# Routed attention and a tanh-shrink feed-forward on one core: third pair's sums copied ahead of weight conversions, list work placed behind weight pieces, products of zeros moved within the prologue

## The chip, the cores and the metric

The kernel runs on one core of a Trainium2 chip. The metric is the device time of one execution in microseconds (us). All times of the trace below are counted from the start of the span of one profiled execution.

## The reference

```python
# q, k, v: (4, 8, 768, 64); centroids: (8, 16, 64); w_in: (512, 2048); w_out: (2048, 512)
q_assign = argmax(einsum('bhsd,hcd->bhsc', q_n, c_n))      # nearest of 16 centroids, normalised
k_assign = argmax(einsum('bhsd,hcd->bhsc', k_n, c_n))
mask = q_assign[:, :, :, None] == k_assign[:, :, None, :]
scores = where(mask, matmul(q, k^T) / sqrt(64), -1e9)
attn = softmax(scores)
x = matmul(attn, v), heads side by side: (3072, 512)
h = x @ w_in
out = (h - tanh(h)) @ w_out
```

The weights arrive as 64-bit floats, two 32-bit words a number, and are converted on the chip.

## The kernel before

Two heads make a pair; there are 4 pairs in each of 4 batches, n = 0 to 15. A pair's 768 queries are cut into two halves of 384, and its 768 keys into three steps s of 256. The main loop runs over 96 such steps (n, half, s): first half 0 of pairs 0 to 3 (steps 0 to 11), then half 1 of the same pairs (12 to 23), then pairs 4 to 15 with both halves in turn. In each step TensorE (PE) makes the scores of the *next* step (`sc`, L451), ScalarE (ACT) takes their exponentials (L473), VectorE (DVE) masks them where the mask isn't already in the product (L483), and PE multiplies with v (`av`, L505). In steps 0 to 11 PE has no feed-forward work; from step 12 the feed-forward of what is finished is dealt out between the steps (`h`, L626; `o`, L642; later `pu`, L818 and `pd`, L869, a seven-product scheme).

The order on every engine is the order in which the Python code issues instructions; nothing reorders it afterwards. Within a step, work that isn't TensorE's main stream is collected in a list `todo`, and `between()` issues it in equal shares between the feed-forward items of the step.

The mask of pairs 1 to 3 in half 0 is a product too (L462) with two one-hot tiles `hot`. To get them, the cluster codes of a pair (`route`, from `pr` L364) are transposed (`pq`, L396), written to memory (`q_codes`, SyncE's queue, SP, L402), read back into 128 partitions (`hot`, L418) and compared on DVE (L426, L430). For unmasked steps the codes come back as `row` (L409), which the masking on DVE (L483) reads.

A half of a pair needs the sums of its weights. `total` copies them from PSUM to a tile `den` on ACT (L544). From there two ways lead on:

- Pairs for which `soon(n)` holds (the third and fourth of the first batch, and the fourth of each other): PE multiplies `den` by a matrix that picks one row out (`tally`, L598, in `pick`, first batch's half 0), DVE takes reciprocals (L603) and scales `xT` (L606).
- The others go through memory, in stages of later steps: `total` also writes the sums (`list`, SP, L553); one step on `compact` reads them as 128x6 (`each`, `other`, L566); two steps on `invert` adds and inverts on DVE (L574, L575) and writes `back` (L577); three steps on `spread_out` reads `back` into `den` (L582); five steps on `scale` multiplies `xT` on DVE (L588). For pair 1's half 0 the last three come a step later. These stages stand in a dictionary `later` by step.

The weights come in 32 pieces. GpSimd (POOL) fetches a raw piece (L218), three ahead; `rest_of` prepares half of its words on ACT (L149, L150) and `round_piece` puts a piece together on DVE (L158, L161) and fetches the piece three on. `paces` says how many pieces a step takes. `rest` has two buffers, so that a third `rest_of` waits for the DVE conversion of the piece before the last.

In step 8, (2, 0, 2), the sums of pair 2's half 0 are complete. Before the change `take` (L530) and two `rest_of` are issued first, and `total` of pair 2 only with `todo`.

In the prologue `keep_warm(times)` issues products of zeros (L302), two instructions each on PE, which nothing reads.

Of the kernel before, what the change touches and what calls it, by code (L numbers as in the profile page):

```python
# [58 lines left out]
def kernel(  # L59
# [119 lines left out]
    def fast():  # L179
# [118 lines left out]
        def keep_warm(times: int):  # L298

            ps = ps_f.tile([P, 2 * P], F32, name="warm", tag="f")  # L300
            for _ in range(times):
                nc.tensor.matmul(  # L302
                    ps, lhsT=inverses[:, 0:P], rhs=inverses[:, 0 : 2 * P], start=True, stop=True
                )
# [22 lines left out]
        def turn(n: int, i: int, engine):  # L327

            pt = ps_s.tile([P, 2, 512], F32, name="pt", tag="s")
            x = raw_qk.pop((n, i))  # L330
            for j in range(NCH):
                nc.tensor.transpose(  # L332
                    out=pt[:, j // HCH, (j % HCH) * P : (j % HCH + 1) * P],
                    in_=x[:, j].rearrange("p h d -> p (h d)"), identity=ident,
                )
            pool = turnp0 if n in (2, 3) else turnp
            t = turned[n, i] = pool.tile([P, 2, TB], F32, name=f"t{i}")
            if engine is nc.scalar:
                nc.scalar.copy(out=t, in_=pt[:, :, 0:TB])
            else:  # L340
                nc.vector.tensor_copy(out=t, in_=pt[:, :, 0:TB])
# [49 lines left out]
        def publish(n: int):  # L391

            sides = 2 if masked(n, 0) else 1
            G = HCH * 4 * sides
            ps = ps_f.tile([G, P], F32, name="pq", tag="f")
            nc.tensor.transpose(  # L396
                out=ps, in_=codes[n][:, 0:sides].rearrange("p i a h j -> p (i a h j)"), identity=ident
            )
            t = rtp.tile([G, P], BF16, name=f"qc{sides}")
            nc.vector.tensor_copy(out=t, in_=ps)  # L400
            q_codes[n] = dram.tile([sides, 2, 2, HCH * P], BF16, name=f"q_codes{sides}")
            nc.sync.dma_start(q_codes[n].rearrange("i a h (j p) -> (i a h j) p", p=P), t)  # L402
# [591 lines left out]
        centroid_load()  # L994
        load(0)
        constants()
        keep_warm(9)
        centroid_norms()

        gate = const.tile([P, 1], F32, name="gate")  # L1000
# [9 lines left out]
        route(0)  # L1010
        turn(1, 0, nc.scalar)
        turn(1, 1, nc.scalar)
        publish(0)
        spread(0, 0)
        rest_of(0)
        similar(1)
        load(2)
        rest_of(1)

# [22 lines left out]


        paces = dict(enumerate((0, 0, 1, 1, 1, 0, 2, 1, 2, 1, 1, 0, 3, 2, 2, 2, 2, 2, 2, 3, 2)))
        late, divides, makers, later = [], [], [], {}
        fill, whole, spent, since, over = [], 0.0, 0.0, 0, 1
        for at, (n, half, s) in enumerate(steps):
            b, p = pairs[n]
            following = steps[at + 1] if at + 1 < len(steps) else None
            after = steps[at + 2] if at + 2 < len(steps) else None  # L1050
            if at == 4 * HALF:
                open_late()
            if at == 4 * HALF - 9:
                open_stream()
            if at in fills:
                fill, over = fills[at][0](), fills[at][1]
                whole, spent, since = sum(it[0] for it in fill), 0.0, at
            if at == 2 * HALF:
                makers = [it for i in range(2) for it in up_maker(i)]
                makers += [it for i in range(2) for it in down_maker(i)]  # L1060
            now = []
            part = (at - since + 1) / over
            while fill and (spent + fill[0][0] / 2 <= whole * part or part == 1):
                now.append(fill.pop(0))
                spent += now[-1][0]
            stages = ready.get(at, {})

            values_first = 1 in stages and not summed(n, half)
            if values_first:
                value(n, half, s)  # L1070
            if 1 in stages:
                stages[1]()
            if after and after[2] == 0 and not masked(*after[:2]):
                spread(*after[:2])
            if following and at >= NS - 1:
                begin(following)
            while picks:
                picks.pop(0)()
            share = paces.get(at, 0)
            todays, rounding = rounding[:share], rounding[share:]  # L1080
            taken = summed(n, half) and s == NS - 1
            if not taken:
                for piece in todays[:2]:
                    rest_of(piece)
            if not values_first:
                value(n, half, s)
            if summed(n, half):
                if 0 in stages:
                    stages.pop(0)()
                sum_up(n, half, s)  # L1090
            if s == NS - 1:
                take(n, half)
                if taken:
                    for piece in todays[:2]:
                        rest_of(piece)
                if soon(n):
                    if summed(n, half):
                        picks.append(lambda n=n, half=half: pick(n, half))
                    divides = [lambda n=n, half=half, i=i: divide(n, half, i) for i in range(HCH)]
                else:  # L1100

                    slow = int((n, half) == (1, 0))
                    for i, stage in (
                        (0, total), (1, compact), (2 + slow, invert), (3 + slow, spread_out),
                        (5 + slow, scale),
                    ):
                        later.setdefault(at + i, []).append(
                            lambda stage=stage, n=n, half=half: stage(n, half)
                        )

                if p == HP - 1 and (half == 1 or b == 0):
                    total(n, half)
                    if summed(n, half):
                        picks += divides
                    else:
                        late += divides
                    divides = []
                if (n, half) == (HP - 1, 0):
                    load(HP)
                if half == 1:  # L1120
                    load(n + (HP if n < 2 else 2), (2,) if n < 2 or n >= HP else ())

            todo = []
            if following:
                todo += [lambda i=i: select(*following[:2], 2 * following[2] + i) for i in range(2)]
            todo += [stages[i] for i in (5, 3, 4, 2) if i in stages]
            todo += late + later.pop(at, [])
            late = []
            if divides:
                todo.append(lambda n=n, half=half: total(n, half))  # L1130
                late, divides = divides, []
            for i, piece in enumerate(todays):
                todo.append(lambda piece=piece: round_piece(piece))
                if i == 0:
                    todo += [lambda piece=piece: rest_of(piece) for piece in todays[2:]]

            light = [i for i in range(at, 4 * HALF - 2) if i % 3 and i % 6 != 1]
            if makers and at in light:
                share = -(-len(makers) // len(light))
                todo += makers[:share]  # L1140
                del makers[:share]
            if "raw" in late_pools:
                todo += [check_done, check_done, check_on, check_on]
                if p == HP - 1 and half == 1 and s == NS - 2:
                    todo += [lambda b=b, c=c: right_factors(b, c) for c in range(CH - 1)]
            slots = max(sum(it[1] for it in now), 1)
            place = iter(range(slots))
            turned_at = max(slots - 1 - now[-1][1], 0) if now else 0

            def between():  # L1150
                i = next(place)
                for it in todo[i * len(todo) // slots : (i + 1) * len(todo) // slots]:
                    it()

                if i == turned_at and 0 in stages:
                    stages[0]()

            if at in fills and "raw" in late_pools:
                for c in range(CH - 1 if at > 4 * HALF else 0, CH):
                    right_factors(b - 1, c)  # L1160
            for it in now:
                it[2](between)
            if not now:
                between()
# [225 lines left out]
```

## Time and profile before

| what | value |
|---|---|
| device time, 3 executions | 987.56, 988.15, 988.5 us; median 988.15 |
| profiled execution | 992.2 us; span of its instructions 990.4 us |
| PE busy | 978.1 us, 99% of the span |
| DVE, ACT, POOL busy | 532.0, 322.0, 499.6 us |
| mean granted TensorE clock | 0.995 |
| mean memory traffic | 134 GB/s |

The slices of the whole span (each digit the busy tenths of one of 40 slices, 24.8 us each) show that PE is full from end to end:

```
PE   8999999999999999999999999999999999999997
DVE  5457557448656667656554357655645336533011
ACT  5566564333442323243331222324341221122000
POOL 1025334444445464776777345676688345466600
PEclk9999999999999999999999999999999999999999
DMA  7656353025475724463536737344453232233231
```

The change touches the first four slices, up to about 90 us, and the order of small work in all later steps. The steps of interest begin, by the scores that they issue for the step after them, at 60.4 us (step 8), 64.9 us (step 9), 73.4 us (step 10), 77.4 us (step 11) and 81.1 us (step 12).

### The profile page before, as it was taken

The page shows a single profiled execution, that of the slowest core. Times are in us where ns is not written, and L with a number is a line of the kernel's source. Part 1 is how long each engine was busy: PE and PEld are TensorE (multiplying, and loading weights), DVE is VectorE, ACT ScalarE, POOL GpSimd, SP SyncE. Part 2 cuts the span into 40 slices and gives each one's busy share as a digit, 9 for nine tenths or more (in the row PEclk, how much of TensorE's full clock was granted, in tenths as well). Part 3 has the DMA queues.
Part 4 walks back from the last instruction along what each step waited for, and adds up shares of the span by engine and source line. Part 5 has one row for each costly group of instructions (what it writes and reads, how often), then busy time and mean ns, then how long its engine had stood idle before and what let it go on. Part 6 is the DMA issues. An engine that isn't in the chain of part 4 may idle for free.

```text
span 990.4 us, 16604 instructions
## 1 busy us (share of the span) xinstructions
PE 978.1 (99%) x6452; PEld 465.8 (47%) x6452; DVE 532.0 (54%) x1019; ACT 322.0 (33%) x493; POOL 499.6 (50%) x347
## 2 busy tenths in 40 slices
PE   8999999999999999999999999999999999999997
PEld 5433443344443334444455555444455555444664
DVE  5457557448656667656554357655645336533011
ACT  5566564333442323243331222324341221122000
POOL 1025334444445464776777345676688345466600
PEclk9999999999999999999999999999999999999999
DMA  7656353025475724463536737344453232233231
GB/s 201 182 143 172 111 177 108 30 51 152 118 222 133 228 92 125 147 174 117 174 113 195 200 116 216 109 147 124 149 166 93 101 110 73 104 112 127 103 102 35
DMA packets 115977, 132.47 MB, mean 134 GB/s; under 512 B 62980, under 2 KB 95668, under 8 KB 113204
## 3 DMA queue, kind: packets, MB, share of 16 engines
q1 hardware_dynamic: 109508, 109.81, 37.5%
q0 software_dynamic: 6240, 21.50, 6.5%
q8 instruction: 53, 0.87, 0.4%
q14 instruction: 32, 0.26, 0.1%
q10 hardware_dynamic: 144, 0.03, 0.0%
HBM read 110.14 MB, written 21.17 MB: 133 GB/s over the span
## 4 chain that ended last, share of the span: by engine, by line
PE 96%; DVE 1%; DMA 1%; ACT 0%; issue 0%; SPq 0%; ACTq 0%; DVEq 0%
PE pd L869 22%; PE pu L818 21%; PE sc L451 14%; PE av L505 14%; PE o L642 8%; PE h L626 8%; PE pt L332 2%; PE den L539 2%; PE sim L351 1%; PE warm L302 1%; DMA den<-back 1%; PE den L520 1%; PE pr L364 1%; DVE e L483 0%; PE pq L396 0%; DMA q_codes<-qc 0%
## 5 line engine op out<-in xcount | busy, mean ns | idle before, releaser
L496 POOL TENSOR_TENSOR sum<-sum,e 128x768 f32<-128x768 f32 x112 | 206.1, 1840 | 106.5 <-DVE e L483 102.7
L483 DVE SCALAR_TENSOR_TENSOR e<-row,code,sc 128x384 f32<-128x384 bf16 x336 | 185.2, 607 | 97.2 <-ACT sc L473 74.3
L869 PE MATMUL pd<-stream,G 128*64 128x256 f32 x1728 | 191.8, 379 | 0.0
L473 ACT ACTIVATE sc<-sc 128x768 f32<-128x768 f32 x168 | 125.8, 792 | 202.3 <-PE sc L451 187.9
L869 PEld LDWEIGHTS pd<-stream,G 128*64 128x64 f32 x1728 | 123.7, 137 | 67.4 <-issue 7.9
L451 PE MATMUL sc<-t,t 64*128 64x384 f32 x768 | 151.5, 513 | 0.1
L505 PE MATMUL av<-e,vals 128*64 128x384 f32 x768 | 146.4, 501 | 0.0
L813 POOL TENSOR_TENSOR G<-G,th 128x768 f32<-128x768 f32 (+1 forms) x51 | 88.0, 1739 | 98.7 <-ACT th L811 98.7
L818 PE MATMUL pu<-xT,stream 128*64 128x384 f32 x768 | 134.9, 488 | 0.7 <-DVE top L372 0.7
L818 PE MATMUL pu<-diff,stream 128*64 128x384 f32 x576 | 103.1, 487 | 0.0
L451 PEld LDWEIGHTS sc<-t,t 64*128 64x128 f32 x768 | 66.6, 188 | 74.6 <-issue 41.7
L492 POOL TENSOR_TENSOR sum<-e 128x768 f32<-128x768 f32 x28 | 56.8, 2029 | 75.8 <-DVE e L483 67.5
L818 PEld LDWEIGHTS pu<-xT,stream 128*64 128x64 f32 x768 | 54.1, 137 | 69.6 <-issue 62.2
L505 PEld LDWEIGHTS av<-e,vals 128*64 128x64 f32 x768 | 47.8, 137 | 82.7 <-issue 80.8
L626 PE MATMUL h<-xT,w_in 128*64 128x384 f32 x512 | 86.3, 487 | 0.0
L642 PE MATMUL o<-w_out,g 128*64 128x512 f32 x384 | 86.3, 594 | 0.0
L811 ACT ACTIVATE th<-G 128x768 f32<-128x768 f32 (+1 forms) x51 | 40.8, 805 | 117.9 <-DVE G L806 112.1
L818 PEld LDWEIGHTS pu<-diff,stream 128*64 128x64 f32 x576 | 40.7, 137 | 49.9 <-issue 44.5
L806 DVE TENSOR_TENSOR G<-pu,u 128x384 f32<-128x384 f32 x72 | 39.7, 552 | 41.4 <-PE pu L818 41.2
L626 PEld LDWEIGHTS h<-xT,w_in 128*64 128x64 f32 x512 | 36.4, 137 | 46.2 <-issue 45.1
L642 PEld LDWEIGHTS o<-w_out,g 128*64 128x64 f32 x384 | 27.0, 137 | 50.3 <-issue 49.6
L880 DVE SCALAR_TENSOR_TENSOR c<-pd,du 128x256 f32<-128x256 f32 x36 | 15.1, 420 | 62.9 <-PE pd L869 62.9
(127 smaller groups left out, 840.7 us busy)
## 6 DMA issues: line engine op xcount, KB each, us to landing
stream<-up_factors SPq DMA_DIRECT2D x24, 896.0 KB
stream<-down_factors SPq DMA_DIRECT2D x21, 1024.0 KB
raw<-in_moe_w_in_dram POOLq DMA_DIRECT2D x16, 512.0 KB, 6.1
raw<-in_moe_w_out_dram POOLq DMA_DIRECT2D x16, 512.0 KB, 5.0
again<-in_moe_w_in_dram SPq DMA_DIRECT2D x32, 256.0 KB
again<-in_moe_w_out_dram SPq DMA_DIRECT2D x32, 256.0 KB
x<-in_q_dram SPq DMA_DIRECT2D x32, 192.0 KB
x<-in_k_dram SPq DMA_DIRECT2D x32, 192.0 KB
```

The source lines that it names most:

```text
L451: nc.tensor.matmul(sc[i][:, h, 0:TB], lhsT=turned[n, 1][r].rearrange("p a n -> p (a n)")[:, j * P : (j + 1) * P], rhs=turned[n, 0][r, half ...
L473: nc.scalar.activation(out=out, in_=sc[i][:, :, 0:TB], func=ACT.Exp, scale=SCALE)
L483: nc.vector.scalar_tensor_tensor(out=e[:, h], in0=rows[n, half][:, h], scalar=codes[n][:, 1, j // HCH, h, j % HCH : j % HCH + 1], in1=sc[: ...
L492: nc.gpsimd.tensor_tensor(out=s, in0=pair[0], in1=pair[1], op=ALU.add)
L496: nc.gpsimd.tensor_tensor(out=s, in0=s, in1=pair[i], op=ALU.add)
L505: nc.tensor.matmul(avs[n, half][h * D : h * D + D], lhsT=vals[n][:, h, j], rhs=e[i][:, h], start=(j == 0), stop=(j == NCH - 1),)
L626: nc.tensor.matmul(h[r], lhsT=w_in[i][:, c, o * P : (o + 1) * P][:, r], rhs=xT[c][:, half], start=(c == 0), stop=(c == CD - 1),)
L642: nc.tensor.matmul(acc[sub][r], lhsT=gs[f % HF][:, f // HF, sub * P : (sub + 1) * P][:, r], rhs=w_out[f // FQ][:, f % FQ], start=(f == seq ...
L811: nc.scalar.activation(out=th, in_=t, func=ACT.Tanh)
L813: nc.gpsimd.tensor_tensor(out=t, in0=t, in1=th, op=ALU.subtract)
L818: nc.tensor.matmul(ps[r], lhsT=streams[base + i][:, c, k_, r], rhs=right[c], start=(c == 0), stop=(c == CH - 1),)
L869: nc.tensor.matmul(ps[r], lhsT=left(i)[:, r], rhs=t[:, i], start=(i == 0), stop=(i == HF - 1))
```

## The change

Three parts, in the prologue and in the main loop.

1. In step 8, where `taken` and `soon(n)` hold, `total` is issued directly behind `take`, ahead of the two `rest_of` that follow. `total` of the step is then not put into `todo` again. (For step 11 the call moves within the same block, without other instructions between.)
2. The stages of `later` are split: `total` (stage 0) stays at its place in `todo`; `compact`, `invert`, `spread_out` and `scale` go to a list `listed` that is appended behind the step's `round_piece` calls.
3. `keep_warm(9)` becomes `keep_warm(7)`; `keep_warm(3)` is added between the transposes of pair 1 and `publish(0)`, and `keep_warm(1)` behind `similar(1)`.

```diff
         constants()
-        keep_warm(9)
+        keep_warm(7)
         centroid_norms()
...
         turn(1, 1, nc.scalar)
+        keep_warm(3)
         publish(0)
         spread(0, 0)
         rest_of(0)
         similar(1)
+        keep_warm(1)
         load(2)
...
-            taken = summed(n, half) and s == NS - 1
+            taken = s == NS - 1 and summed(n, half)
...
                 if taken:
+                    if soon(n):
+                        total(n, half)
                     for piece in todays[:2]:
                         rest_of(piece)
...
                 if p == HP - 1 and (half == 1 or b == 0):
-                    total(n, half)
                     if summed(n, half):
                         picks += divides
                     else:
+                        total(n, half)
                         late += divides
                     divides = []
...
-            todo += late + later.pop(at, [])
+            todo += late
             late = []
             if divides:
-                todo.append(lambda n=n, half=half: total(n, half))
+                if not taken:
+                    todo.append(lambda n=n, half=half: total(n, half))
                 late, divides = divides, []
+
+            for it in later.pop(at, []):
+                if it[0] == 0:
+                    todo.append(it[1])
+                else:
+                    listed.append(it[1])
             for i, piece in enumerate(todays):
                 todo.append(lambda piece=piece: round_piece(piece))
                 if i == 0:
                     todo += [lambda piece=piece: rest_of(piece) for piece in todays[2:]]
+            todo += listed
+            listed = []
```

Beside the intended moves the order of instructions differs thus: on SP, for 17 of the 22 halves that go through memory, the two reads of `back` (L582) now stand behind the writes of the next half's `list` (L553) in place of ahead of them; on PE the product `den` (L539) stands one feed-forward item earlier in five places; on DVE `invert` and `scale` of the first batch stand behind one to three conversions. POOL's order is the same. PE executes two products of zeros (four instructions) more in all.

More of the change, by code (lines that the diff above doesn't have):

```diff
@@ L1044, in fast @@
         paces = dict(enumerate((0, 0, 1, 1, 1, 0, 2, 1, 2, 1, 1, 0, 3, 2, 2, 2, 2, 2, 2, 3, 2)))
-        late, divides, makers, later = [], [], [], {}
+        late, divides, makers, later, listed = [], [], [], {}, []
         fill, whole, spent, since, over = [], 0.0, 0.0, 0, 1
@@ L1107, in fast @@
                         later.setdefault(at + i, []).append(
-                            lambda stage=stage, n=n, half=half: stage(n, half)
+                            (i, lambda stage=stage, n=n, half=half: stage(n, half))
                         )
                 if p == HP - 1 and (half == 1 or b == 0):
-                    total(n, half)
                     if summed(n, half):
```

## Prediction

> **What bounds the kernel now.** I read the engine table first (PE busy 978.1 of 990.4 us), then the chain of waits and PE's own waits. The kernel is a TensorE stream; only places where PE stands still or runs slowly can give time back.
>
> ```profile
> PE 96%; DVE 1%; DMA 1%; ACT 0%; issue 0%; SPq 0%; ACTq 0%; DVEq 0%
> ...
> PE tally L598 <- ACT den L544: 2.0, 1, 2.0
> PE warm L302 <- DVE inverses L231: 1.3, 1, 1.3
> PE pq L396 <- DVE code L377: 1.2, 1, 1.2
> PE pu L818 <- DVE top L372: 0.7, 2, 0.3
> PE pr L364 <- ACT simt L356: 0.7, 1, 0.7
> ```
>
> The second block names who PE waited for (sum, count, longest in us): three waits can be won, 2.0 at the third pair's `tally`, 1.2 and 0.7 in the prologue. The chain of waits, in order of time (start, length), shows what stands behind the first:
>
> ```profile
> 57.78 7.32 DMA den<-back
> ...
> 65.19 0.56 DVE xT L588
> ...
> 68.35 0.34 ACT den L544
> ...
> 68.73 1.37 PE tally L598 x4
> 70.11 2.57 PE av L505 x8
> 72.68 0.78 PE den L520 x8
> 73.46 1.49 PE sc L451 x8
> ...
> 82.70 0.79 PE tally L598 x4
> 83.50 1.44 PE av L505 x8
> ```
>
> A list read (`den<-back`) holds DVE at `scale` of pair 0 until 65.19; the conversions behind it come late; ACT's second `rest_of` waits for a buffer; `den` of pair 2 stands behind it on ACT, and PE behind `den`. The last two rows are the same PE work undisturbed: after the wait it ran 0.58 and 1.13 us longer. Four stretches of one clock window each say why (busy PE, granted clock):
>
> ```profile
> 14.34:17.75 3.41, 1.55 (x14) 1.00 0.13 50
> 17.75:21.16 3.41, 3.41 (x13) 0.50 0.47 124
> 65.54:68.95 3.41, 1.43 (x12) 1.00 0.24 65
> 68.95:72.37 3.42, 3.42 (x12) 0.50 0.58 149
> ```
>
> A window in which PE idled 1.86 or 1.98 of 3.41 us was followed by one at half clock.
>
> [...] PE's `den` product had ended at 64.93 (64.08 + 0.85), yet ACT copied it at 68.22. [...] a `row` read issued at 71.97 landed only at 78.55, behind raw pieces that landed at 75.6 and 77.3; an undisturbed one took 17.64 to 20.79.
>
> **The change part by part**, against the span of 990.4.
>
> *Third pair's sums.* ACT's order becomes xT (to 64.68), `den`, then the two `rest_of`. `den` can run at 64.97 to 65.45. PE's next scores end at 66.75, so `tally` waits for nothing: 1.98 us gone, and with it the half clock, 0.58 + 1.13. Together 3.7 us here (`sc` of step 10 at 69.8, not 73.5). The `rest_of` behind it start 0.45 later (65.46, not 65.01); the exponentials queued behind them, which free the banks for `sc`, come at 68.3 instead of 68.58, because the second `rest_of` no longer waits 0.54 for DVE. They end at 69.8, just as PE arrives. So this part gains 2.0 where the half-clock window is missing, 3.7 where it is not. [...] Mean: 1.99 + 0.5 x 1.71 = 2.85.
>
> *List work behind weight pieces.* On DVE the conversion of step 7 runs at 62.2 to 63.4 inside the 3.04 us in which DVE waited for the list. What it costs: `den<-back` of pair 0 is issued behind four `list` writes (1.26 us on SP), so about 58.4 instead of 57.13; `scale` starts at 65.2 to 66.4 (both bounds: nothing later, as the DMA engines were full of raw pieces until 64, or the whole 1.26), I take 65.8. Nobody but the feed-forward at 84.8 needs it. Pair 1's `invert` then comes behind two conversions, the second of which waits for ACT (68.15): conversions end at 68.9, `back` is issued at 69.4, not 67.24. SP waits for its landing (3.5 us before), then issues `den<-back`, then `row` for step 12: about 74.2 instead of 71.97. This `row` matters. Step 12's four maskings (2.2), `scale` (0.55), three reciprocals (2.57) and xT (0.56) follow it on DVE, 5.95 us, and the fourth product group of the first `h` needs that xT, 86.79 before. With PE earlier by g, `row` must have landed by 86.79 - 5.95 - g = 80.8 - g, i.e. 78.0 for g = 2.85. When does it land? Earliest 74.2 + 3.15 = 77.4 (the undisturbed latency), latest 74.2 + 6.6 = 80.8 (the latency of before). The raw pieces in its way are fetched some 1.5 us earlier than before, since conversions are, so I take 78.3. That is a stall of 0.3 at the mean; as lateness costs and earliness gives nothing, I charge 0.8. Net of both parts: 2.85 - 0.85 = 2.0.
>
> The other 17 moved `den<-back` reads go behind `list`, which waits for ACT; `scale` follows two steps, over 16 us, later (the steps' scores lie 8 to 10 us apart), and the slowest read took 7.3. Cost nothing, hidden by the feed-forward. Behind them on SP stand loads that stood behind `list` anyway. The five `den` products that move up one item (1.29 or 3.4 us) read sums that POOL had finished 2.7 us or more before: nothing. POOL keeps its order.
>
> *Products of zeros.* The rows show starts 0.427 us apart for an instruction while cold and 0.21 once warm. Two products fewer are four instructions; the last began at 8.14 and `pc` at 8.36; now the stream ends at 7.46, `pc`'s inputs being there at 7.01 and the k load at 7.07: 0.9 earlier here. With windows elsewhere the gain lies between 0 (early warm, `pc` waits for its inputs) and 1.3; mean 0.5. The three products before `pq` are 6 x 0.213 = 1.28 us in a gap of 1.205: `pq` may come 0.1 late. If PE were cold there, 2.56, late by 1.4. The one behind `sim` takes 0.43 of a gap of 0.66: nothing. In exchange the half-clock window at 17.75 goes: `sc` took 2.89 where others take 1.49, `pr` 0.65 for 0.48, so 1.57. [...] Mean of the part: 0.5 - 0.1 + 0.14 x 1.57 = 0.6. In this very trace it would be 2.4, of which the one-hot read limits some: `hot` landed at 32.57 and PE met it at 33.6, while its codes queue behind loads that move only 0.75.
>
> *Sum.* 2.0 + 0.6 = 2.6 us. The profiled span (990.4) and execution (992.2) lie above the three timed ones (987.56 to 988.5), perhaps with more half-clock windows; that is why I use means over positions. 988.15 - 2.6 = 985.5.
>
> **Rivals.** About 0.2% (2.0 us) is what can be told from no change.
>
> A, likeliest: the wait goes, a part comes back at `row`. 985.5; its own range 983.8 to 986.5. Chance 0.60.
>
> B, the wait moves: `row` lands at 79.5 or later and PE stops 1.5 at the first `h`, or the three products delay `pq` by 1.4. Gain 2.85 - 1.5 + 0.6 - 0.9 (half of the clock's 1.71, if that hole is taken for idleness too) = 1.05: 987.1. For it: 1.5 us of SP and DVE work really moves ahead of `row`, and before it `row` had only 0.7 us to spare (78.55, masking at 79.28). Against: raw pieces move away from it. Chance 0.24.
>
> C, nothing comes back and both half-clock windows were there: 3.7 + 1.3 = 5.0, so 983.2. Against: the timed runs are below the profiled one. Chance 0.10.
>
> D, slower: the same `row`, pushed behind a raw piece, lands at 82 or later. PE then waits 82 - 77.1 = 4.9 at `h` (with g = 3.7), idles over 1.86 in a window, and the next 3.41 us at half clock cost 1.7: 6.6 lost against 3.7 + 0.6 won, 990.4. It decides from about 79.7, where stall and clock equal the gain, and is slower by more than 0.2% from 81.7. Against: 82 is 7.8 us after the issue, more than any read of this kind took. Chance 0.06.
>
> That the change doesn't do what it says is inside B: the products may not lie in idle time.
>
> **Numbers.** Faster by over 0.2%: 0.55 of A, all of C, 0.02 of B = 0.67; within: 0.05 of A, 0.22 of B = 0.27; slower 0.06. Range 983.0 to 987.5: it takes A, half of C and most of B, leaving out about 0.15. All cases but D have one sign.
>
> **What would show it.** PE's waits no longer list `tally` on ACT `den`; `den` of pair 2 runs on ACT within 1 us of PE's product; no half-clock window follows; `sc` of step 10 comes within 3.2 us of `sc` of step 9's end. Wrong, if PE has a new wait at `h` on DVE xT or at `av` on DVE `e` near step 12 (B, D), if DVE waits at L483 for `row`, or if `pc` doesn't start before 8. A time above 987.5 with no such wait would mean that the holes cost less outside the profile than in it.

## The result, and the profile after

The changed kernel is slower: 994.85 us (median of 6 executions, 993.9 to 997.52) against 988.33 us (6 executions, 987.56 to 990.79) for the kernel before on the same chip. The ratio is 1.0063, with a 95% interval of 1.0046 to 1.0081. The forecast was 985.5 us, with a range up to 987.5: wrong in sign. The profiled execution of the kernel after took 994.45 us, its span 992.7; before, the span was 990.4.

First, the share of the span by what the chain of waits ran through, and who PE waited for (sum, count, longest, in us), after:

```profile
PE 95%; DMA 2%; DVE 1%; issue 0%; ACT 0%; SPq 0%; ACTq 0%; DVEq 0%
...
PE sc L451 <- DVE e L483: 5.1, 1, 5.1
PE warm L302 <- DVE inverses L231: 1.3, 1, 1.3
PE pt L332 <- issue: 0.9, 2, 0.8
PE pu L818 <- DVE top L372: 0.7, 2, 0.3
```

The three waits that were to be won (`tally`, `pq`, `pr`) are gone. In their place stands one of 5.1 us, at a `sc` that waits for the masking on DVE. DVE's own waits say what the masking waited for (of the two waits in the sum, the longest is this one):

```profile
DVE e L483 <- DMA row<-q_codes: 8.2, 2, 5.5
```

The chain of waits after, in order of time (start, length), goes back from that `sc` through the read of `row` and the write of `back` to the weight conversions on DVE and ACT, and from there to the list read of pair 0:

```profile
57.51 5.70 DMA den<-back
...
63.23 0.57 DVE xT L588
...
66.28 0.64 ACT rest L150
...
67.55 0.17 DVE each L574
...
67.75 0.20 DVE each L575
...
67.96 4.54 DMA back<-each
...
73.65 6.04 DMA row<-q_codes
...
80.31 0.62 DVE e L483
...
81.07 2.93 PE sc L451 x8
84.00 1.48 PE tally L598 x4
85.48 1.44 PE av L505 x8
```

To be read off: pair 1's inverses (`each`, L574 and L575) run behind the conversions; their write `back` takes 4.54 us; `row`, which SP issues only behind it, takes 6.04; PE goes on 1.38 us after `row` has landed (79.69 to 81.07), 0.13 behind the end of the second masking (80.94): the next scores go to the place in PSUM that these two maskings read, and the profile names the masking for PE's 5.1 us. `sc` and the `tally` of the fourth pair then take 2.93 and 1.48 where undisturbed ones took 1.49 and 0.79. Stretches of 3.41 us with PE's work and granted clock say why; up to 90 us the half clock lasted twice 3.41 us in the profile of before, and here once 6.83, from 78.63 to 85.46 (stretch, length, busy PE, granted clock, DMA share, GB/s):

```profile
13.76:17.17 3.41, 3.38 (x21) 1.00 0.26 104
17.17:20.59 3.42, 3.15 (x19) 1.00 0.60 148
71.79:75.20 3.41, 3.41 (x28) 1.00 0.30 81
75.20:78.63 3.43, 0.76 (x8) 1.00 0.78 205
78.63:82.04 3.41, 0.97 (x4) 0.50 1.16 297
82.04:85.46 3.42, 3.42 (x14) 0.50 0.65 136
```

In the prologue the half-clock window is gone. The stop at step 12 fills most of two windows (2.67 and 2.44 us without PE work), and the next one of each is at half clock. `sc` and `tally` take (2.93 - 1.49) + (1.48 - 0.79) = 2.1 us longer than undisturbed ones. Not all of that is the clock's: in two kernels below that stop there without a half clock (part 2 alone, and the zeros in the wait), `sc` takes 1.97 us; in the first it runs in two halves of 0.92 us with 0.13 between them. That the second half waits for the third and fourth masking is the author's reading. So the stop costs 5.1 us of waiting and 0.5 of this kind, and the half clock (2.93 - 1.97) + (1.48 - 0.79) = 1.65.

Where the 2.3 us between the two spans arose can be followed by landmarks. `pc` begins at 7.21 (before 8.36), the third pair's `tally` at 65.12 (68.73), the fourth's at 83.93 (82.64), the first `h` at 86.75 (84.77), the first `o` at 149.44 (147.46), the last `pd` at 986.43 (984.1). A lead of 3.6 us at 65 is a lag of 2.0 at 87, and hardly anything changes behind that. All of it lies between the two `tally` products, and the other 900 us need not be looked at. This holds for every kernel below: in all fourteen profiles 905.4 to 906.0 us pass from the start of the first `h` to the end of the span.

Two timelines show the mechanism. SP's queue after (start, time on the queue):

```profile
67.96 0.32 SPq L577 DMA_DIRECT2D back<-each  x1
72.52 1.09 SPq L582 DMA_DIRECT2D den<-back  x2
73.65 0.59 SPq L409 DMA_DIRECT2D row<-q_codes  x1
```

And POOL's fetches of raw weight pieces after, 512 KB each:

```profile
65.95 0.57 POOL L218 DMA_DIRECT2D raw<-in_moe_w_in_dram  x1 [0.50 <-ACT rest L150]
67.29 0.53 POOL L218 DMA_DIRECT2D raw<-in_moe_w_in_dram  x1 [0.77 <-ACT rest L150]
72.80 0.74 POOL L218 DMA_DIRECT2D raw<-in_moe_w_in_dram  x1 [0.83 <-ACT rest L150]
73.97 0.53 POOL L218 DMA_DIRECT2D raw<-in_moe_w_in_dram  x1 [0.43 <-issue]
```

Each conversion ends by fetching the piece three on. Since the list work now stands behind the conversions, it also stands behind their fetches: two pieces are sent 2.0 and 0.7 us ahead of `back`, and two more 0.85 us ahead of `row` and 0.3 us after it. In the profile of before the second fetch of the two came 2.5 us *after* `back`.

### The profile page after: what moved, and what is told of

Same layout as the page of the kernel before. It is cut to its first block, busy times and chain, and to the rows that moved or that the text cites. A ratio compares the mean times of both kernels' runs of the same rounds, so it can differ in the third digit from the quotient of the medians.

```text
span 992.7 us, 16628 instructions
## 1 busy us (share of the span) xinstructions
PE 977.9 (99%) x6456; PEld 465.8 (47%) x6456; DVE 530.5 (53%) x1019; ACT 321.8 (32%) x493; POOL 500.6 (50%) x347
## 4 chain that ended last, share of the span: by engine, by line
PE 95%; DMA 2%; DVE 1%; issue 0%; ACT 0%; SPq 0%; ACTq 0%; DVEq 0%
PE pd L869 22%; PE pu L818 21%; PE sc L451 14%; PE av L505 13%; PE o L642 8%; PE h L626 8%; PE pt L332 2%; PE den L539 2%; PE sim L351 1%; PE warm L302 1%; PE pr L364 1%; DMA row<-q_codes 1%; DMA den<-back 1%; DVE e L483 1%; PE den L520 0%
## 5 line engine op out<-in xcount | busy, mean ns | idle before, releaser
L483 DVE SCALAR_TENSOR_TENSOR e<-row,code,sc 128x384 f32<-128x384 bf16 x336 | 185.2, 607 | 101.0 <-ACT sc L473 72.1
```

The costliest lines, as they stand in the source:

```text
L483: nc.vector.scalar_tensor_tensor(out=e[:, h], in0=rows[n, half][:, h], scalar=codes[n][:, 1, j // HCH, h, j % HCH : j % HCH + 1], in1=sc[: ...
```

## The experiments

Each kernel was timed beside the kernel before on the same chip; the diffs are shortened. "Wait at step 12" is PE's wait at the `sc` that is issued as step 12 begins, from the run's profile. Parts 1, 2 and 3 are those of the change.

**The parts alone.** Part 1 alone, put on the kernel before (with `total` not put into `todo` a second time):

```diff
                 if taken:
+                    if soon(n):
+                        total(n, half)
                     for piece in todays[:2]:
```

> Only the third pair's sums are moved; lists and zeros as before. Row theory (the loss is the `row` read of step 12, which stands on SP behind `back` and `den<-back` of pair 1, and the list part pushes these back): the tally wait of 2.0 us goes, `row` keeps its place in time (landing near 78.5), PE, up to 3.7 earlier, waits 0.5 to 2.4 at the scores of step 12; 986.5 to 988.5. Lead theory (any lead of PE runs into a read that comes at a fixed time, and the stop brings the half clock; the list part is innocent): a wait of over 3 us at the scores of step 12 with the half clock behind it, 990 or more.

Measured: 987.48 us (14 executions) against 988.06, ratio 0.9993 (0.9983 to 1.0004), as the row theory had it. No wait at `tally`; a wait of 1.0 at step 12. Here `back` is issued at 65.35, ahead of the conversions of its step, and SP sends the next reads 1.99 us later. So the wait that part 1 removes comes back in part at step 12, even where the list work stays where it was, and little is won.

Part 2 alone, on the kernel before:

```diff
-            todo += late + later.pop(at, [])
+            todo += late
...
+            for it in later.pop(at, []):
+                if it[0] == 0:
+                    todo.append(it[1])
+                else:
+                    listed.append(it[1])
...
+            todo += listed
```

> Only the list stages are put behind the weight pieces; sums and zeros as before. Row theory: `back` of pair 1 about 2 us later against PE, `row` with it, a wait of 1 to 2 us at the scores of step 12 beside a tally wait that stays at 1.5 to 2.0: 988.8 to 991. Lead theory: PE gains nothing, so no wait at step 12: 988.3, within 0.5.

Measured: 992.51 us (6 executions) against 988.06, ratio 1.0046 (1.0032 to 1.0059): slower without any help from the other parts, and by more than the row theory had expected. PE's waits in its profile:

```profile
PE sc L451 <- DVE e L483: 2.5, 1, 2.5
PE warm L302 <- DVE inverses L231: 1.3, 1, 1.3
PE pq L396 <- DVE code L377: 1.2, 1, 1.2
PE tally L598 <- ACT den L544: 0.9, 1, 0.9
```

The old wait stays and the new one is added. `row` was issued at 73.53 and the first masking ran at 79.28. No half clock followed the new wait: behind it each half of `sc` took 0.92 us and `tally` 0.79. By the author's count the idleness was spread over two windows, 1.12 and 1.56 us.

Part 3 alone, on the kernel before:

```diff
-        keep_warm(9)
+        keep_warm(7)
...
+        keep_warm(3)
...
+        keep_warm(1)
```

> Only the products of zeros are moved. Both theories: the prologue is 0.5 to 2 us shorter, everything behind it shifts together, `row` too; no wait at step 12: 986.3 to 988. A third theory, that the products themselves cost time (6.5 us lost are theirs): 990 or more.

Measured: 987.29 us against 988.06, ratio 0.9992 (0.9984 to 1.0). The prologue's waits at `pq` and `pr` are gone, but in this profile `pt` waits 1.5 us until 26.46. The profile names ACT's copy `t` for it, which had ended 0.67 us before; more likely it was the load of pair 2's `x`, met by a PE that comes earlier, but this isn't shown.

**Row read early.** The changed kernel, with step 12's `row` read issued in step 8, ahead of `back`:

```diff
+            if at == 8:
+                spread(0, 1)
-            if after and after[2] == 0 and not masked(*after[:2]):
+            if after and after[2] == 0 and not masked(*after[:2]) and at != 10:
                 spread(*after[:2])
```

> The changed kernel, with the `row` read of step 12 issued two steps earlier (in step 8, ahead of `back` of pair 1 on SP), which nothing prevents, as the codes of pair 0 have been in memory since 17 us. Row theory: the wait of 5.1 us at the scores of step 12 and the half clock behind it go; at most 1 us remains at the first `h`, for the list read of pair 1: 984 to 986. If something else on DVE or the memory queues is the cause, the wait stays over 3 us and the time over 990.

Measured: 987.29 us against 988.06, ratio 0.9994 (0.9986 to 1.0002), and no wait at step 12. `row` went out at 62.54; `back` still took 4.11 us and hurt nobody. The whole loss stands or falls with the landing of `row`. The time expected was 984 to 986: curing step 12 brings back the time of the kernel before, and no more.

**Clock or wait.** The changed kernel, with eight products of zeros put into the stop at step 12, so that PE isn't idle while it waits:

```diff
+            if at == 12:
+                keep_warm(8)
```

> The changed kernel with eight further products of zeros (3.4 us at the full clock) in the wait before the scores of step 12, so that PE stands still for 1.7 us less long and the `row` read comes no earlier. If the half clock behind the wait is a part of the loss of its own: the wait stays as dead time, scores and tally behind it run at 1.5 and 0.8 us again, 1.5 to 2.2 us less than the changed kernel (994.85): 992.6 to 993.4. If the wait alone is the loss: 994.3 to 995.5.

Measured: 992.35 us (4 executions, 991.58 to 993.17) against 987.54, ratio 1.0053 (1.0038 to 1.0068). In the profile the zeros fill 3.7 us, a wait of 1.8 is left, and the granted clock from 80 to 90 us is 1.00:

```profile
80.00 1.97 PE L451 MATMUL sc<-t,t 64*128 64x384 f32 x8 [1.84 <-DVE e L483]
```

From the first masking to the first `h` it is 5.31 us here (78.72 to 84.03) and 6.97 in the changed kernel (79.78 to 86.75): 1.66 less, which agrees with the 1.65 read above. The timed executions give 1.0 us by the ratios, whose intervals overlap, so they don't settle the size. The rest of the loss is the wait.

**The change without part 2:**

```diff
-            todo += late
+            todo += late + later.pop(at, [])
```

> The changed kernel without its list part. Row theory with the list part as the cause: `row` lands as early as in the kernel with the sums alone, the wait at step 12 is 1 to 2.5 us, 986 to 988. Lead theory: both parts that give PE a lead are in, so the wait is that of the changed kernel (5 us) and the time over 992.

Measured: 987.15 us against 987.54, ratio 0.9998 (0.9989 to 1.0007); wait at step 12 0.8 us. PE arrives as early here as in the changed kernel (74.88 for 75.96), and isn't stopped for 5 us: that PE comes too soon is not the cause. SP's queue in it:

```profile
65.14 0.32 SPq L577 DMA_DIRECT2D back<-each  x1
67.36 1.09 SPq L582 DMA_DIRECT2D den<-back  x2
68.49 0.59 SPq L409 DMA_DIRECT2D row<-q_codes  x1
```

`row` lands at 74.33 here, after 5.84 us, and at 79.69 in the changed kernel. Of these 5.4 us, 2.8 come from the later issue of `back`, 2.3 from its taking 4.56 us in place of 2.22, and only 0.2 from `row` itself.

**Inverses first.** The changed kernel, with pair 1's `invert` alone back ahead of the conversions of its step:

```diff
-                if it[0] == 0:
+                if it[0] == 0 or at == 8:
                     todo.append(it[1])
```

> The changed kernel, with one stage put back: pair 1's `invert` in step 8 ahead of the two weight pieces on DVE, as before the change; everything else, the order on SP too, stays. If the place of `invert` is what delays `row`: `back` is issued 3 us earlier, `row` follows, the wait at step 12 falls under 1.5 us and the half clock goes: 986.5 to 989. If the order on SP or the crowding of the memory queues by raw pieces is the cause: over 992.

Measured: 987.12 us against 987.54, ratio 0.9992 (0.9984 to 1.0), no wait at step 12. SP's queue in it:

```profile
63.36 0.32 SPq L577 DMA_DIRECT2D back<-each  x1
64.78 1.09 SPq L582 DMA_DIRECT2D den<-back  x2
65.92 0.59 SPq L409 DMA_DIRECT2D row<-q_codes  x1
```

One of the moved stages makes the whole loss, and the order on SP, which is that of the changed kernel, has no part in it. `back` goes out 4.6 us earlier than in the changed kernel, but it also takes only 1.4 us in place of 4.56: of the 7.7 us by which `row` is issued earlier, 3.1 are due to the write being quicker. This left open which of the two counts, the earlier issue or a road without raw pieces in flight.

**No part of the zeros.** The changed kernel without part 3:

```diff
-        keep_warm(7)
+        keep_warm(9)
...
-        keep_warm(3)
...
-        keep_warm(1)
```

> The changed kernel with the products of zeros as before (sums and lists stay). If the zeros have no part in the loss: 993.5 to 995.5, the wait at step 12 at 4 to 5.5 us. If the shorter prologue is what sharpens it: 991 to 993, the wait under 3.5.

Measured: 994.43 us (4 executions) against 987.54, ratio 1.0075 (1.0054 to 1.0095), wait at step 12 5.0 us, half clock from 78.16 to 84.99 (mean granted clock 0.995, as in the changed kernel). The zeros have no part in the loss.

**The kernel before again**, unchanged, profiled twice more, one execution each:

> The kernel before, profiled a second time, to see how much of the 2.0 us wait at the tally and of the half clock behind it belongs to the one execution that the prediction was worked out on. If that execution was typical: a tally wait of 1.8 to 2.1. If not: a wait of 0.8 to 1.3, as in the kernels with the lists or the zeros alone, no half-clock window in the first 100 us and a span of 985 to 987.

> A third profile of the kernel before, to the same end: a tally wait of 1.8 to 2.1 if the first execution was typical, 0.8 to 1.3 if it was not.

Measured: 990.17 and 989.5 us, spans 988.4 and 987.7. PE's wait at the third `tally`, first in the one and then in the other:

```profile
PE tally L598 <- ACT den L544: 1.5, 1, 1.5
```

```profile
PE tally L598 <- ACT den L544: 0.9, 1, 0.9
```

The profile from which the forecast was made had 2.0 there and a half-clock window behind it; these two have no such window. What was to be won at `tally` was 0.9 to 1.5 us in them, not 3.7. The 1.5 lies between the two ranges that were set, and the spans lie above the one expected. Both do have the half-clock window of the prologue (from 17.24 and 17.78 us), which that expectation had excluded.

**Raw pieces held back.** The changed kernel, `invert` still behind the conversions, but the fetches of raw pieces 11 to 13 held to the end of step 9's list, behind `invert` (a conversion of step 10 moves to step 13 for it; behind L227 the lines of this kernel are numbered one higher):

```diff
-            fetch(at + AHEAD)
+            if at not in (8, 9, 10):
+                fetch(at + AHEAD)
...
-        paces = dict(enumerate((0, 0, 1, 1, 1, 0, 2, 1, 2, 1, 1, 0, 3, 2, 2, 2, 2, 2, 2, 3, 2)))
+        paces = dict(enumerate((0, 0, 1, 1, 1, 0, 2, 1, 2, 1, 0, 0, 3, 3, 2, 2, 2, 2, 2, 3, 2)))
...
+            if at == 9:
+                todo += [lambda: fetch(8 + AHEAD), lambda: fetch(9 + AHEAD), lambda: fetch(10 + AHEAD)]
```

> The changed kernel, with the fetches of raw pieces 11 to 13 held back on POOL until pair 2's inverses are added (about 72 us instead of 66, 67 and 73), and the piece of step 10 converted in step 13. `invert` stays behind the two conversions. If raw pieces in flight are what stretches the small write of `back` (4.6 us from issue to the next issue) and the `row` read: `back` takes 1.5 to 2.5 us, the wait at step 12 falls to 0.5 to 3 us, 989 to 991.5. If the place of `invert` alone sets it, without the crowding: the wait stays over 4 us, 993 or more.

Measured: 987.55 us against 987.33, ratio 0.9999 (0.9991 to 1.0008), and no wait for `row` at step 12, better than either range expected. SP's queue, and then POOL's fetches:

```profile
66.97 0.32 SPq L578 DMA_DIRECT2D back<-each  x1
68.38 1.10 SPq L583 DMA_DIRECT2D den<-back  x2
69.52 0.59 SPq L410 DMA_DIRECT2D row<-q_codes  x1
```

```profile
60.26 0.53 POOL L218 DMA_DIRECT2D raw<-in_moe_w_in_dram  x1 [3.74 <-issue]
70.91 1.62 POOL L218 DMA_DIRECT2D raw<-in_moe_w_in_dram  x3
```

`back` goes out only 1.0 us earlier than in the changed kernel (66.97 for 67.96), takes 1.41 us for 4.56, and the first masking runs at 73.50 for 79.78, so that `row` took at most 3.98 us. Of the 6.28 us, 1.0 come from the issue, 3.1 from `back` and 2.1 from `row`: five of six from a road without raw pieces ahead. Either cure is enough alone, so the loss needs both: `invert` behind the conversions, and their fetches ahead of `back` and `row`.

**Both cures for step 12.** The changed kernel with the edits of "inverses first" and "row read early" together:

> The changed kernel with both cures: pair 1's `invert` ahead of the pieces, and the `row` read of step 12 issued in step 8. Row theory: no wait at step 12; as the kernel with the first cure has none left either, the same time within 0.5 us: 986.3 to 987.3, below the kernel before by 0.5 to 1.5 us.

Measured: 987.08 us (21 executions) against 987.33, ratio 0.9992 (0.9985 to 0.9999), as expected. No wait of PE is left at step 12, at `tally`, `pq` or `pr`; the longest is 1.3 us, for the zeros' own input at the start.

It is quicker than the changed kernel, and than the one before by some 0.8 us (0.08%) by the ratio, whose interval just leaves out no difference (by the medians 0.25 us); the first cure alone has the same ratio. Its profiled span is 983.5, 4.2 to 6.9 below the three profiles of before; its timed executions are spread over 985.36 to 988.98, and the profiled one was the quickest. Why the timed gain is so much smaller than the spans suggest isn't settled. Part of it is that the profiled executions of before (989.5 to 992.2) lie high among its timed ones: all three have the half-clock window of the prologue, which costs some 1.6 us, and nothing shows how many of the timed ones have it. Part may be waits at `pt` that come in some executions only: three of the eight profiles with part 3 have one, of 0.8, 1.5 and 2.2 us (changed kernel, part 3 alone, row read early).

## Why the prediction was wrong

**What bounds the kernel; what would show it.** Right. The three waits were the ones named, and the loss again is one place at which PE stands still. The signs listed held: `tally` waits for nothing, `den` ran on ACT at 63.87, within 1 us of PE's product, no half clock followed it, `pc` began before 8. So did one of the signs of being wrong: DVE waits at L483 for `row`. The prediction looked at the right transfer and put a chance of 0.06 on what it did.

**The failed step: when `row` is needed.** The prediction put the deadline at the fourth product group of the first `h`, by way of the chain maskings, reciprocals and `xT`: 80.8 - g, so 78.0 for g = 2.85. In the changed kernel PE stood ready at step 12 at 75.96, so `row` had to land by 75.96 - 1.38 = 74.6. The deadline was taken 3.4 us too late, the largest error of the sum, and it has two causes. PE at step 12, first before and then after:

```profile
80.36 0.85 PE L520 MATMUL den<-e,ones 128*32 128x384 f32 x8
81.14 1.56 PE L451 MATMUL sc<-t,t 64*128 64x384 f32 x8
```

```profile
75.11 0.85 PE L520 MATMUL den<-e,ones 128*32 128x384 f32 x8
81.07 2.93 PE L451 MATMUL sc<-t,t 64*128 64x384 f32 x8 [5.11 <-DVE e L483]
```

The first cause is the reader. `sc` of step 13, issued as step 12 begins, waits until two maskings have read the scores of step 12 (5.11 us here, put down to the masking). In the profile of before that deadline is 81.21 - 1.38 = 79.8, 1.0 us ahead of the 80.8 that was used. The second, and larger, is the lead g. PE was ready at 81.21 before and at 75.96 after: 5.25 us earlier, 2.4 more than the 2.85 put in. The 86.79 from which the deadline was counted was read from an execution in which two half-clock windows had cost PE 1.7 and 1.6 us by then, and the changed kernel had neither on its way to step 12; but g counted half of the first and nothing of the second, nor of part 3. A time of one execution was set against a mean over executions. Even by the prediction's own reader, then, a landing at 79.69 stops PE for 79.69 - (80.84 - 5.25) = 4.1 us. Of the wait of 5.1, 0.3 was forecast, 1.4 is the later landing, 1.0 the reader and 2.4 the lead. This doesn't make the lead the cause: without part 2 `row` keeps up with it and lands at 74.33, and part 2 is what holds `row` back, to 79.69. Beside this two slips hardly count: the four terms of the chain add up to 5.88 us, not 5.95, and the charge of 0.8 stands as 0.85 in the net.

Rival D had the mechanism and the price (4.9 of waiting, 1.7 of clock; 5.1 and 1.65 were measured), but the wrong place and a lead of 3.7, and so the point at which it decides was set at a landing of 79.7, where the wait had already reached its full price.

**The failed argument: raw pieces in the way of `row`.** It was taken that earlier conversions, which fetch raw pieces earlier, move them out of the way. The sign was wrong. Before, the pieces of steps 9 and 10 were sent 3.1 and 6.3 us after `row`; now they are sent 0.85 us ahead of it and 0.3 after it, and both pieces of step 8 go out ahead of `back`, with the list work behind them. The prediction saw that the conversions fetch, but took that for a help to `row`, and took over the time of `back` from the trace of before, without asking what the fetches do to it, though it had read from that trace that a `row` read landed behind raw pieces, 6.58 us after its issue. Of the terms, `back` was taken at 3.5 us and took 4.56; `row` was taken at 4.1 (78.3 - 74.2) and took 6.04, about what it takes in every profile where the masking waits for it (5.66 to 6.89). The issue of `back`, taken at 69.4, came earlier, at 67.96. The landing at 79.69 lay inside the bounds given (77.4 to 80.8), 1.4 late of the value chosen.

**Part 1's gain was mis-sized.** 1.99 of wait and 0.86 of clock at the mean were taken from one profile. Two other profiles of the same kernel have 1.5 and 0.85, and no half clock behind it; and part 1 alone then loses 1.0 at step 12. Measured: 0.6 us (ratio 0.9993, no difference within its interval), where 2.85 was expected. The half of the clock's 1.71 was an estimate of how often the windows lie so that a half clock follows; the runs don't show that share, and it was put on a wait that was itself at the top of its spread.

**Part 3.** Taken at 0.6, measured 0.8 us (0.9992, 0.9984 to 1.0). That the size is right is partly luck. The waits at `pq` and `pr` went, but the zeros only fill them: from `pc` to the second `pr` it is 9.09 us in the changed kernel and 9.08 before. What can be won is the earlier `pc` and the half-clock window behind these waits. That window was given a chance of 14%, an estimate; it stands in four of the six profiles with the old products of zeros (all three of before, and part 2 alone). Against it come the waits at `pt`, which the prediction didn't have.

**The sum as it was.** Without part 2 the change is worth some 0.2 us (0.9998, no difference within its interval). Part 2, charged at little (0.85), costs 1.0063 - 0.9998 = 0.65%, or 6.4 us, give or take 2 by the two intervals. The traces agree: 5.1 - 0.8 = 4.3 us more of waiting at step 12 than without part 2, and 1.65 of clock, together 5.9. Of the stages that part 2 moves, undoing the one `invert` takes the loss away. That the other moved stages cost nothing, as predicted, is shown by the same run, in which they all stay moved (0.9992).

## What to carry to other kernels

When work is moved behind other work, ask what *that* work issues: here two conversions that end with a prefetch put two pieces of 512 KB ahead of a write of 3 KB on another queue, and the write took 4.56 us, where it took 1.41 with the pieces held back. For every transfer that a change delays, list all readers and what each reading frees, the PSUM of the next product among them, and take the earliest as the deadline. Read that deadline and the time set against it from the same execution, and move both with the change. And profile the kernel before more than once before pricing a wait of 2 us: in five profiles in which `tally` waits it is 2.0, 1.5 and three times 0.9, and the best kernel here won 0.8.

## What the runs showed of the hardware that was not expected

The small write of `back` took longer where raw pieces had been sent shortly ahead of it on another queue, 4.08 to 4.59 us with two of them and 1.41 to 1.79 with none. From the issue of `back` (3 KB) to SP's next issue, which waits for it, in all fourteen profiles, by where the nearest raw pieces (512 KB) were sent:

| raw pieces sent, us from `back` | kernels | us |
|---|---|---|
| none from -3.0 to +1.8 | raw pieces held, inverses first, both cures | 1.41, 1.42, 1.79 |
| -1.9, +0.8 | part 1 alone, change without part 2 | 1.99, 2.22 |
| -1.3, +1.9 | before, third profile | 2.43 |
| -0.6, next at +2.5 or later | before (first and second profile), part 3 alone | 3.49, 3.15, 3.36 |
| -0.3, +0.2 | part 2 alone | 3.70 |
| -2.0, -0.7 | changed kernel, zeros in the wait, no part of the zeros, row read early | 4.56, 4.59, 4.08, 4.11 |

Against the 1.4 to 1.8 us with no piece near, it took about half a microsecond longer with one sent 1.9 us ahead, about two with one sent 0.6 us ahead, about three with two sent 2.0 and 0.7 us ahead. Only the run with the fetches held was made to test this; the other rows are what the kernels happened to do.

Some waits of PE were followed by a half clock and others weren't. In the first profile of before, 1.86 and 1.98 us of idleness in a window of 3.41 were followed by half clock, and in the changed kernel 2.67 and 2.44. In the second profile of before, the 1.5 us wait at `tally` lay within one window, and the next stayed at full clock (stretch, length, busy PE, clock, DMA share, GB/s):

```profile
65.02:68.43 3.41, 1.91 (x14) 1.00 0.31 87
68.43:71.84 3.41, 3.41 (x24) 1.00 0.54 172
```

With the zeros in the wait, the 1.66 us of idleness between 78.48 and 81.89 were followed by full clock (1.00 from 80 to 90 us), and so was the wait of 2.5 us with part 2 alone (`tally` 0.79 behind it), whose idleness the author counted as 1.12 and 1.56 us in two windows. These are the waits that were read for it; what between 1.66 and 1.86 us would have done, they don't show.
